# Attention scores in units of two head pairs instead of four heads of one half

## The chip, the cores and the metric

The kernel runs on one core of a Trainium2 chip. The metric is the device time of one execution, in microseconds (us); the median of three runs is given. TensorE is called PE here, VectorE DVE, ScalarE ACT, GpSimd POOL, SyncE SP.

## What is computed

Attention with a band mask and a distance bias, then a feed-forward layer, then an eight-expert layer whose gate is balanced by eight row and column normalisations. The change touches attention alone.

```python
def _attn_ref(q, k, v, n_global, n_local):          # q, k, v: (2, 8, 768, 64) float32
    scores = scale * np.matmul(q, k.transpose(0, 1, 3, 2))
    ...
    keep = is_global | is_local                     # first 8 keys, and the last 96 up to the own one
    bias = -slopes[:, None, None] * dist[None, :, :]
    scores = np.where(keep, scores + bias[None, :, :, :], -1000000000.0)
    a = np.exp(scores - np.max(scores, axis=-1, keepdims=True))
    a = a / (np.sum(a, axis=-1, keepdims=True) + 1e-09)
    return np.matmul(a, v)                          # heads joined: x is (1536, 512)

def _moe_ref(x, w_in, w_out):                       # w_in, w_out: float64
    h = x @ w_in
    return (h * (1.0 / (1.0 + np.exp(-h)))) @ w_out

def _moe2_ref(x, w_gate, w1, w2):
    ...                                             # gate P: exp, then 8 normalisations
    for e in range(E):
        out += P[:, e:e + 1] * (np.maximum(x @ w1[e], 0.0) @ w2[e])
```

## The kernel before, in words

**Attention.** The 1536 tokens are twelve query tiles k of 128. A tile needs 256 keys at most (`W`; 32 places for the global ones and 224 before and up to the query), the first tile of a batch 128. `att_turn` (line 660) transposes a tile's queries and keys on PE, two heads at a time, so that `qT` and `kT` hold the even head of a pair (j = 0) on partitions 0 to 63 and the odd one (j = 1) on partitions 64 to 127. There are four pairs (c). A score product contracts over the 64 rows of one half.

`att_scores(k, j)` (line 708) is a unit: the four heads of half j. For two of them, c and c + 1, it takes one PSUM bank, issues their score products (line 726), and then for each head: DVE adds the table of bias and mask and takes the row's minimum (line 735, tile `s`; the sign of the scores is turned, so that the minimum stands for the maximum), ACT takes the exponential and its sum (line 739); after both heads DVE makes the reciprocals (lines 744 and 745) and POOL scales (line 747). Then it yields. `att_flip` (line 752) transposes a unit's weights on PE, up to four blocks a bank (line 764, tile `a_f`), and copies them to `at`. `att_out` (line 776) multiplies them with the values for a whole tile (line 783, tile `a_o`), and its two copies write x as a rounded part `xh` and a rest `xl`.

Tiles 0 to 7 use fp32 operands (one product for a head, which the trace shows as two matmul records). For tiles 8 to 11 queries and keys are split into a rounded part and a rest, and a head takes three products in fp32r (`qT·kT`, `qT·kTl`, `qTl·kT`), one record each.

**PSUM.** While attention runs there are three banks of tag `a` for all its tiles, taken in turn, one `h` and four `y` (line 846). In the first two tiles the `y` banks serve too.

**Order.** `attention` (line 797) is a generator: each step issues one piece (half a unit's scores, one bank of flips, an `att_out`, a part of a turn). Flips run two units behind the scores (`LAG`). `go` (line 892) runs the first feed-forward layer (`emit_h`, lines 237 to 239 and 256 to 260; `emit_y`, line 276) and lets the generator make a piece each time that its due count reaches one. Each step of that layer is an h (12 matmuls) and a y (12) over 512 tokens; the first token block starts with four steps of half width, twice. The order within an engine is then fixed; the build has moved instructions a little against the order in which the code issues them. Tiles 0 and 1 run ahead of the layer, 2 and 3 in its first steps, 4 to 7 in the rest of token block 0, 8 to 11 in block 1. Block 2 and the second layer (`h_product`, `y_part`) have no attention beside them.

**The weights of block 0.** `w_in` and `w_out` come as float64; `narrow` (line 183) turns a slice of them into fp32 by eight DVE instructions (lines 199 to 205), handed out by `pump` between other work on the same DVE queue. From line 212 on ACT and POOL split them for PE. Blocks 1 and 2 load the fp32 copy.

Of the kernel before, what the change touches and what calls it, by code (L numbers as in the profile page):

```python
# [8 lines left out]
F32 = mybir.dt.float32  # L9
# [5 lines left out]
AF = mybir.ActivationFunctionType  # L15
ALU = mybir.AluOpType
# [4 lines left out]
P = 128  # L21
# [3 lines left out]
W = 2 * P  # L25
BIG = float(2**40)
BIGMIN = 3.0e38
MASKED = 1.0e9
EPS = 1e-9
# [5 lines left out]
LAG = 2  # L35
# [7 lines left out]
def f32(ap):  # L43
    return ap.bitcast(F32)


class Kernel:
# [657 lines left out]
                nc.vector.scalar_tensor_tensor(dst[1], ps, sc, f32(dst[0]), op0=ALU.mult, op1=ALU.subtract)  # L705
            yield

    def att_scores(self, k, j):

        nc, pool = self.nc, self.ap  # L710
        a = self.att[k]
        qT, kT = a["qT"], a["kT"]
        n = W if k % self.QT else P
        jj = slice(j * self.D, (j + 1) * self.D)
        a["s", j] = s = pool.tile([P, 4, W], F32, tag="s", name=f"s_{k}_{j}", bufs=LAG + 1)
        st = pool.tile([P, 3, 4], F32, tag="st", name=f"st_{k}_{j}", bufs=LAG + 2)
        cols = []
        for c in range(self.NPAIR):
            th = self.tab[2 * c + j]
            if c % 2 == 0:  # L720
                bank = self.aps(f"s_{k}_{j}_{c}")
                for x in (c, c + 1):
                    dst = bank[:, x % 2 * W:x % 2 * W + n]
                    ops = ((0, 0), (0, 1), (1, 0))[:3 if len(qT) > 1 else 1]
                    for i, (y, z) in enumerate(ops):
                        nc.tensor.matmul(  # L726
                            dst, qT[y][jj, x * P:(x + 1) * P], kT[z][jj, x, W - n:],
                            start=i == 0, stop=i == len(ops) - 1,
                        )
            ps = bank[:, c % 2 * W:c % 2 * W + n]  # L730
            tt = th[:, :W] if n == W else th[:, W:]
            sx = s[:, c, W - n:]
            cols.append(sx)

            nc.vector.tensor_tensor_reduce(  # L735
                out=sx, in0=ps, in1=tt, scale=1.0, scalar=BIGMIN, op0=ALU.add, op1=ALU.min,
                accum_out=st[:, 0, c:c + 1],
            )
            nc.scalar.activation(
                sx, sx, AF.Exp, bias=st[:, 0, c:c + 1], scale=-1.0, accum_out=st[:, 1, c:c + 1]  # L740
            )
            if c % 2 == 1:
                two = slice(c - 1, c + 1)
                nc.vector.tensor_scalar(st[:, 2, two], st[:, 1, two], EPS, None, op0=ALU.add)  # L744
                nc.vector.reciprocal(st[:, 2, two], st[:, 2, two])
                for y in (c - 1, c):
                    nc.gpsimd.tensor_scalar(
                        cols[y], cols[y], st[:, 2, y:y + 1], 1.0, op0=ALU.mult, op1=ALU.mult
                    )
                yield  # L750

    def att_flip(self, k, j):

        nc, pool = self.nc, self.ap
        a = self.att[k]
        s, blocks = a["s", j], self.blocks(k)
        at = a["at", j] = pool.tile([P, 8 * P], F32, tag="at", name=f"at_{k}_{j}", bufs=2)
        for lo in range(0, len(blocks), 4):
            hi = min(lo + 4, len(blocks))
            ps = self.aps(f"f_{k}_{j}_{lo}")  # L760
            for n in range(lo, hi):
                c, o = blocks[n]
                keys = s[:, c, P:] if o is None else s[:, c, o::2]
                nc.tensor.transpose(ps[:, (n - lo) * P:(n - lo + 1) * P], keys, self.ident)  # L764
            if lo == 0:
                nc.scalar.activation(at[:, :hi * P], ps[:, :hi * P], AF.Copy)
            else:
                self.copy(at[:, lo * P:hi * P], ps[:, :(hi - lo) * P])
            yield

    def blocks(self, k):


        return [(c, o) for c in range(self.NPAIR) for o in ((0, 1) if k % self.QT else (None,))]

    def att_out(self, k):

        nc = self.nc
        a = self.att.pop(k)
        ps = self.aps(f"o_{k}")  # L780
        for n, (c, o) in enumerate(self.blocks(k)):
            for j in range(2):
                nc.tensor.matmul(  # L783
                    ps[j * self.D:(j + 1) * self.D, c * P:(c + 1) * P], a["vw"][:, 2 * c + j, o or 0, :],
                    a["at", j][:, n * P:(n + 1) * P], start=n == 0, stop=o != 0, skip_group_check=True,
                )
        tok = k * P
        xh, xl = (x[:, :, tok % TB:tok % TB + P] for x in self.x1[tok // TB])
        ps = ps.rearrange("p (x c) -> p x c", c=P)
        nc.scalar.activation(xh, ps, AF.Copy)  # L790
        nc.vector.tensor_tensor(xl, ps, f32(xh), op=ALU.subtract)
# [5 lines left out]
    def attention(self, sg):  # L797

        tb = SEGS[sg][0] * P // TB
        if tb not in self.x1:  # L800
            self.x1[tb] = self.new_x(f"x1_{tb}")
        ks = range(*SEGS[sg])
        units = [(k, j) for k in ks for j in range(2)]
        if "qT" not in self.att[ks[0]]:
            yield from self.turn(ks[0])
        none = iter(())
        for u in range(len(units) + LAG + 1):
            v = u - LAG
            if v >= 2 and v % 2 == 0:
                k = units[v - 2][0]  # L810
                self.att_out(k)
                if k + 2 < self.NT // P:
                    self.att_load_v(k + 2)
                yield
            if u % 2 == 0 and u + 2 < len(units):
                yield from self.turn(units[u + 2][0])
            scores = self.att_scores(*units[u]) if u < len(units) else none
            flip = self.att_flip(*units[v]) if 0 <= v < len(units) else none
            n = 1
            while n:  # L820
                n = 0
                for g in (scores, flip):
                    for _ in g:
                        n += 1
                        yield
                        break
# [323 lines left out]
```

## Time and profile before

| | |
|---|---|
| median of 3 runs | 1442.73 us (1442.69 to 1444.27) |
| the profiled execution's own time | 1444.39 us |
| its span, first to last instruction | 1442.6 us |
| mean granted TensorE clock | 0.989 of full |
| PE busy | 1413.3 us, 98% |
| DVE / ACT / POOL busy | 739.9 (51%) / 487.2 (34%) / 553.6 us (38%) |
| score matmuls (line 726) | 224 records, 10.2 to 289.5 us |

The span is read in stretches: 0 to 34 us is tiles 0 and 1 before the layer; to about 158 us the layer's first token block with the narrowing of weights beside it; to about 310 us the rest of attention under the layer; then there is no attention. Matmuls are pipelined, so a matmul's record is longer than its share of the array: the distance between the starts of two matmuls is what the first one costs the stream.

### The profile page before, as it was taken

To read this page: it belongs to the slowest core of one execution; us is meant where nothing else is said; L and a number is where in the kernel's file an instruction comes from. 1 tells how busy PE (TensorE), PEld (TensorE's weight loads), DVE (VectorE), ACT (ScalarE), POOL (GpSimd) and SP (SyncE) were. 2 spreads that over 40 slices of the span, in tenths; PEclk is the share of its full clock that TensorE was granted. 3 is DMA by queue.
4 is the path that set the end of the run, shared out by engine and by line. 5 is a ranking of instruction groups with operands and counts; after the bars stand their busy time and mean duration, and the time that the engine had idled before them with its cause. 6 is when DMAs were issued, how large, how long until landed. Compare 5 with 4: busy or idle time off the path is not lost.

```text
span 1442.6 us, 21250 instructions
## 1 busy us (share of the span) xinstructions
PE 1413.3 (98%) x8552; PEld 1232.1 (85%) x8552; DVE 739.9 (51%) x1298; ACT 487.2 (34%) x949; POOL 553.6 (38%) x489
## 2 busy tenths in 40 slices
PE   8998999999999999999999999999999999999998
PEld 6776687778888989999998999899899899989997
DVE  8899545456353556544354354435444443544443
ACT  6665545555352422222232221223222132322220
POOL 5677755444470423314142331414224141422210
PEclk8899999999999999999999999999999999999999
DMA  9685442222230201011010101102010110201001
GB/s 257 178 245 186 154 121 73 74 74 88 88 103 1 59 1 59 16 44 41 19 50 10 59 16 44 44 16 57 3 59 22 38 45 15 59 0 45 1 28 63
DMA packets 75292, 92.18 MB, mean 64 GB/s; under 512 B 30640, under 2 KB 49072, under 8 KB 75184
## 3 DMA queue, kind: packets, MB, share of 16 engines
q1 hardware_dynamic: 72880, 82.34, 19.2%
q10 hardware_dynamic: 2304, 8.39, 1.5%
q8 instruction: 69, 1.13, 0.3%
q14 instruction: 39, 0.32, 0.1%
HBM read 79.19 MB, written 11.53 MB: 63 GB/s over the span
## 4 chain that ended last, share of the span: by engine, by line
PE 89%; DVE 8%; issue 1%; ACT 1%; POOL 0%; DMA 0%; DVEq 0%; ACTq 0%; SPq 0%; POOLq 0%
PE y L423 37%; PE h L388 32%; PE y L276 7%; PE h L237 3%; PE h L238 3%; PE h L239 3%; PE a_s L726 2%; DVE wf L201 1%; DVE wf L203 1%; DVE wf L199 1%; DVE wf L205 1%; PE a_o L783 1%; PE a_f L764 1%; DVE s L735 1%; DVE st L744 0%
## 5 line engine op out<-in xcount | busy, mean ns | idle before, releaser
L480 DVE TENSOR_TENSOR tabs<-tabs,h 128x512 f32<-128x512 f32 x48 | 33.0, 687 | 333.9 <-PE h L388 333.9
L343 POOL TENSOR_TENSOR wc0l<-wf,wc0h 128x512 fp32r<-128x512 f32 x16 | 21.2, 1323 | 340.3 <-ACT wc0h L342 340.3
L440 DVE SCALAR_TENSOR_TENSOR x<-y,gate,x 128x512 f32<-128x512 f32 x168 | 115.5, 742 | 18.3 <-PE y L423 18.3
L343 POOL TENSOR_TENSOR wx1l<-wf,wx1h 128x512 fp32r<-128x512 f32 x64 | 89.9, 1405 | 79.7 <-ACT wx1h L342 79.5
L402 ACT ACTIVATE room_hh<-tabs 128x512 fp32r<-128x512 f32 x87 | 54.2, 629 | 190.9 <-DVE tabs L410 188.5
L410 DVE TENSOR_TENSOR tabs<-tabs,h 128x512 f32<-128x512 f32 x144 | 98.8, 687 | 19.0 <-PE h L388 16.8
L343 POOL TENSOR_TENSOR wx0l<-wf,wx0h 128x512 fp32r<-128x512 f32 x48 | 62.1, 1293 | 90.3 <-ACT wx0h L342 90.3
L388 PE MATMUL h<-xc,wx1h 128*128 128x256 f32 x512 | 93.4, 280 | 1.7 <-DVE tabs L410 1.7
L388 PE MATMUL h<-xc,wx0h 128*128 128x256 f32 x512 | 93.4, 280 | 0.6 <-DVE tabs L476 0.6
L423 PE MATMUL y<-wx1h,room_hh 128*128 128x512 f32 x232 | 91.2, 393 | 0.0
L423 PE MATMUL y<-wx0h,room_hh 128*128 128x512 f32 x232 | 91.2, 393 | 0.0
L423 PE MATMUL y<-wx0l,room_hh 128*128 128x512 f32 x232 | 90.8, 391 | 0.0
L423 PE MATMUL y<-wx1l,room_hh 128*128 128x512 f32 x232 | 90.8, 391 | 0.0
L423 PE MATMUL y<-wx0h,room_hl 128*128 128x512 f32 x232 | 90.7, 391 | 0.0
L423 PE MATMUL y<-wx1h,room_hl 128*128 128x512 f32 x232 | 90.7, 391 | 0.0
L403 DVE SCALAR_TENSOR_TENSOR room_hl<-tabs,room_hh 128x512 fp32r<-128x512 f32 x87 | 77.6, 898 | 25.5 <-ACT room_hh L402 24.2
L342 ACT ACTIVATE wx1h<-wf 128x512 fp32r<-128x512 f32 x64 | 40.4, 632 | 141.8 <-PE y L423 84.2
L388 PEld LDWEIGHTS h<-xc,wx0h 128*128 128x128 f32 x512 | 82.6, 188 | 5.8 <-DVE tabs L476 0.8
L221 POOL TENSOR_TENSOR w1l<-wf,w1h 128x512 fp32r<-128x512 f32 x48 | 67.0, 1395 | 50.9 <-ACT w1h L220 44.6
L388 PEld LDWEIGHTS h<-xc,wx1h 128*128 128x128 f32 x512 | 80.4, 188 | 4.4 <-DVE tabs L410 1.9
L221 POOL TENSOR_TENSOR w0l<-wf,w0h 128x512 fp32r<-128x512 f32 x48 | 67.0, 1397 | 42.0 <-ACT w0h L220 40.2
L276 PE MATMUL y<-hh,w1h 128*128 128x512 f32 (+1 forms) x208 | 83.0, 399 | 0.0
(270 smaller groups left out, 4143.3 us busy)
## 6 DMA issues: line engine op xcount, KB each, us to landing
wf<-in_moe_w_dram SPq DMA_DIRECT2D x64, 512.0 KB, 3.7
wf<-w SPq DMA_DIRECT2D x32, 512.0 KB, 3.3
ra<-in_moe_w_in_dram SPq DMA_DIRECT2D x16, 512.0 KB, 6.0
rb<-in_moe_w_out_dram SPq DMA_DIRECT2D x16, 512.0 KB, 5.3
w<-wf ACTq DMA_DIRECT2D x16, 512.0 KB, 4.3
vw<-in_v_dram SPq DMA_DIRECT2D x8, 448.0 KB, 4.5
qr<-in_q_dram SPq DMA_DIRECT2D x12, 256.0 KB, 5.8
kr<-in_k_dram SPq DMA_DIRECT2D x12, 256.0 KB, 6.0
```

Of the source, the lines that this page charges most:

```text
L221: nc.gpsimd.tensor_tensor(lo, src, f32(hi), op=ALU.subtract)
L237: nc.tensor.matmul(ps, ah, bh, start=i == 0, stop=False)
L238: nc.tensor.matmul(ps, ah, bl, start=False, stop=False)
L239: nc.tensor.matmul(ps, al, bh, start=False, stop=i == last)
L276: nc.tensor.matmul(self.y[i][:, cols], a, b, start=begin and j == 0, stop=f == self.NF1 - 1 and j == 2, skip_group_check=True,)
L343: self.nc.gpsimd.tensor_tensor(dst[1], src, f32(dst[0]), op=ALU.subtract)
L388: nc.tensor.matmul(ps[:, f * HB:(f + 1) * HB], a[:, k, fs], b[:, k, :], start=first and n == 0, stop=n == 11, skip_group_check=True,)
L402: self.nc.scalar.activation(hi, src, AF.Relu)
L403: self.nc.vector.scalar_tensor_tensor(lo, src, 0.0, f32(hi), op0=ALU.max, op1=ALU.subtract)
L410: self.nc.vector.tensor_tensor(c, a, b, op=op)
L423: nc.tensor.matmul(self.y[i], a, b, start=k == 0 and j == 0, stop=k == 3 and j == 2, skip_group_check=True)
L440: nc.vector.scalar_tensor_tensor(acc, self.y[i], self.gate[:, t, e:e + 1], acc, op0=ALU.mult, op1=ALU.add)
```

## The change

A unit is now two pairs: `att_scores(k, m)` takes the heads of c = 2m and 2m + 1, both halves. It takes two banks at once, one for each half; a bank holds the two heads of its half side by side. All score products of the unit are issued in one piece, and two products of the two halves take turns: for each c and each of its one or three products first j = 0, then j = 1. The reductions then go pair by pair: x = 0 reads both banks, x = 1 again, with a yield after each. The first piece of a unit so holds all its matmuls and two heads' reductions, the second piece the other two heads' reductions and no matmul. `att_flip` and `blocks` count heads of the unit instead of pairs; `att_out` visits the same 16 (or 8) products, ordered by c, key block and j as before, and takes the blocks of c from unit c // 2. The number of instructions of each kind is the same.

```diff
-    def att_scores(self, k, j):
+    def att_scores(self, k, m):
...
-        jj = slice(j * self.D, (j + 1) * self.D)
...
-        for c in range(self.NPAIR):
-            th = self.tab[2 * c + j]
-            if c % 2 == 0:
-                bank = self.aps(f"s_{k}_{j}_{c}")
-                for x in (c, c + 1):
-                    dst = bank[:, x % 2 * W:x % 2 * W + n]
-                    ops = ((0, 0), (0, 1), (1, 0))[:3 if len(qT) > 1 else 1]
-                    for i, (y, z) in enumerate(ops):
-                        nc.tensor.matmul(
-                            dst, qT[y][jj, x * P:(x + 1) * P], kT[z][jj, x, W - n:],
-                            start=i == 0, stop=i == len(ops) - 1,
-                        )
...
+        banks = [self.aps(f"s_{k}_{m}_{j}") for j in range(2)]
+        dst = [bank[:, x * W:x * W + n] for x in range(2) for bank in banks]
+        ops = ((0, 0), (0, 1), (1, 0))[:3 if len(qT) > 1 else 1]
+        for x in range(2):
+            c = 2 * m + x
+            for i, (y, z) in enumerate(ops):
+                for j in range(2):
+                    jj = slice(j * self.D, (j + 1) * self.D)
+                    nc.tensor.matmul(
+                        dst[2 * x + j], qT[y][jj, c * P:(c + 1) * P], kT[z][jj, c, W - n:],
+                        start=i == 0, stop=i == len(ops) - 1,
                     )
-                yield
+        for x in range(2):
+            for h in (2 * x, 2 * x + 1):
+                th = self.tab[4 * m + h]
+                sx = s[:, h, W - n:]
+
+                nc.vector.tensor_tensor_reduce(
+                    out=sx, in0=dst[h], in1=th[:, :W] if n == W else th[:, W:], scale=1.0, scalar=BIGMIN,
+                    op0=ALU.add, op1=ALU.min, accum_out=st[:, 0, h:h + 1],
+                )
...
+            yield
...
     def att_out(self, k):
...
+        for c in range(self.NPAIR):
+            for o in range(keys):
+                for j in range(2):
+                    n = (c % 2 * 2 + j) * keys + o
+                    nc.tensor.matmul(
+                        ps[j * self.D:(j + 1) * self.D, c * P:(c + 1) * P], a["vw"][:, 2 * c + j, o, :],
+                        a["at", c // 2][:, n * P:(n + 1) * P], start=c + o == 0, stop=o == keys - 1,
+                        skip_group_check=True,
+                    )
...
-        units = [(k, j) for k in ks for j in range(2)]
+        units = [(k, m) for k in ks for m in range(2)]
```

**PE, first unit of tile 9 (fp32r, beside y of the layer).** In `a_s_0_0` the first number is the unit; the second is, before, the pair with which the bank begins, and now the half. Before, with the second group of the unit 16 rows further on:

```order
L239 MATMUL h_2415<-x_1xh,w0l_2159 128x512
L726 MATMUL a_s_0_0_2447<-kT_2218,qT_2217 128x256
L726 MATMUL a_s_0_0_2447<-kTl_2220,qT_2217 128x256
L726 MATMUL a_s_0_0_2447<-kT_2218,qTl_2219 128x256
...
L764 MATMUL a_f_0_0_2476<-ident,s_0_2276 128x128 x4
...
L726 MATMUL a_s_0_2_2492<-kT_2218,qT_2217 128x256
L726 MATMUL a_s_0_2_2492<-kTl_2220,qT_2217 128x256
L726 MATMUL a_s_0_2_2492<-kT_2218,qTl_2219 128x256
...
L764 MATMUL a_f_0_4_2523<-ident,s_0_2276 128x128 x4
```

Now:

```order
L239 MATMUL h_2415<-x_1xh,w0l_2159 128x512
L725 MATMUL a_s_0_0_2447<-kT_2218,qT_2217 128x256
L725 MATMUL a_s_0_1_2448<-kT_2218,qT_2217 128x256
L725 MATMUL a_s_0_0_2447<-kTl_2220,qT_2217 128x256
L725 MATMUL a_s_0_1_2448<-kTl_2220,qT_2217 128x256
L725 MATMUL a_s_0_0_2447<-kT_2218,qTl_2219 128x256
L725 MATMUL a_s_0_1_2448<-kT_2218,qTl_2219 128x256
...
L761 MATMUL a_f_0_0_2483<-ident,s_0_2276 128x128 x4
...
L761 MATMUL a_f_0_4_2523<-ident,s_0_2276 128x128 x4
```

Two groups of six in one half have become one group of twelve in which the halves take turns; each head's three products stand twice in a group, for two heads. The program has 45 runs of score products before and 25 now. All eight units of tiles 8 to 11 look like this one.

**PE, tiles 2 and 3 (fp32, beside the first steps of the layer).** The build has put other work between some turns. Before, the score rows alone:

```order
L726 MATMUL a_s_0_0_566<-kT_484,qT_483 128x256 x2
...
L726 MATMUL a_s_0_2_581<-kT_484,qT_483 128x256 x2
L726 MATMUL a_s_1_0_606<-kT_484,qT_483 128x256
...
L726 MATMUL a_s_1_2_625<-kT_484,qT_483 128x256 x2
L726 MATMUL a_s_0_0_646<-kT_512,qT_511 128x256
```

Now, from the second run on:

```order
L725 MATMUL a_s_0_1_567<-kT_484,qT_483 128x256
L725 MATMUL a_s_0_0_566<-kT_484,qT_483 128x256
...
L725 MATMUL a_s_1_0_606<-kT_484,qT_483 128x256
L725 MATMUL a_s_1_1_607<-kT_484,qT_483 128x256
...
L725 MATMUL a_s_0_0_646<-kT_512,qT_511 128x256 x2
...
L725 MATMUL a_s_0_1_647<-kT_512,qT_511 128x256 x2
```

The runs of tiles 2 and 3 hold 2, 3, 4, 1, 2, 1, 1 and 2 heads before and 1, 3, 6, 2 and 4 now; the first unit of tile 3 is torn into its halves, and so is that of tile 4.

**DVE, first unit of tile 2.** Before:

```order
L735 ISA s_0_564,st_0_565<-a_s_0_0_566,tabs 128x256
...
L203 SCALAR_TENSOR_TENSOR wf_554<-ra_330,wf_554 128x512
L257 SCALAR_TENSOR_TENSOR g_523<-g_523,h_474 128x256
L735 ISA s_0_564,st_0_565<-a_s_0_2_581,tabs 128x256
```

Now:

```order
L257 SCALAR_TENSOR_TENSOR g_523<-g_523,h_474 128x256
L734 ISA s_0_564,st_0_565<-a_s_0_0_566,tabs 128x256
...
L734 ISA s_0_564,st_0_565<-a_s_0_1_567,tabs 128x256
...
L203 SCALAR_TENSOR_TENSOR wf_554<-ra_333,wf_554 128x512
```

Two reductions, a narrowing instruction and the layer's g, and two more reductions have become g and four reductions in a row, with the narrowing behind them.

## Rows read from the trace of the kernel before

**Rows 1.** The page, parts 1 and 4: busy time of the engines, and the chain that ended last.

```profile
PE 1413.3 (98%) x8552; PEld 1232.1 (85%) x8552; DVE 739.9 (51%) x1298; ACT 487.2 (34%) x949; POOL 553.6 (38%) x489
...
PE 89%; DVE 8%; issue 1%; ACT 1%; POOL 0%; DMA 0%; DVEq 0%; ACTq 0%; SPq 0%; POOLq 0%
```

**Rows 2.** Table by stretch: length, busy time of each engine, clock, DMA.

```profile
40.00:58.00 18.00, 18.00 (x90) 14.06 (x90) 14.65 (x52) 13.02 (x41) 13.44 (x18) 0.81 0.72 197
58.00:158.00 100.00, 89.86 (x550) 70.71 (x549) 94.08 (x189) 59.62 (x145) 71.25 (x68) 0.97 0.65 198
158.00:200.00 42.00, 40.98 (x224) 32.52 (x223) 11.02 (x30) 22.78 (x47) 27.80 (x29) 1.00 0.41 134
200.00:220.00 20.00, 20.00 (x101) 15.56 (x100) 17.29 (x42) 12.06 (x30) 12.76 (x18) 1.00 0.44 114
220.00:320.00 100.00, 98.93 (x570) 79.03 (x569) 49.73 (x125) 51.84 (x117) 46.83 (x55) 1.00 0.24 75
```

**Rows 3.** Waits of PE from 158 to 420 us: total, times, longest.

```profile
PE h L237 <- DVE g L257: 2.1, 2, 1.1
```

**Rows 4.** Timeline of PE, one fp32r group of tile 11: start, us, what.

```profile
273.37 0.40 PE L276 MATMUL y<-hh,w1l 128*128 128x512 f32 x1
273.69 0.38 PE L726 MATMUL a_s<-kT,qT 64*128 64x256 f32 x1
273.92 0.28 PE L726 MATMUL a_s<-kTl,qT 64*128 64x256 f32 x1
...
274.40 0.28 PE L726 MATMUL a_s<-kT,qTl 64*128 64x256 f32 x1
274.61 0.50 PE L276 MATMUL y<-hh,w1h 128*128 128x512 f32 x1
274.94 0.39 PE L276 MATMUL y<-hl,w1h 128*128 128x512 f32 x1
275.17 0.39 PE L276 MATMUL y<-hh,w1l 128*128 128x512 f32 x1
```

**Rows 5.** Line 726, the product with kTl: shortest/median/longest ns, first and last start.

```profile
L726 PE MATMUL a_s<-kTl,qT x32: 277/277/281, 206.5 to 289.4; 64*128 64x256 f32 x32
```

**Rows 6.** Timeline of PE, one fp32 group of tile 7.

```profile
160.15 0.40 PE L239 MATMUL h<-x_0xh,w0l 128*128 128x512 f32 x1
160.48 1.13 PE L726 MATMUL a_s<-kT,qT 64*128 64x256 f32 x4
...
161.88 0.39 PE L238 MATMUL h<-x_0xl,w0h 128*128 128x512 f32 x1
```

**Rows 7.** Timeline of PE, an fp32 group of four records and one of six.

```profile
57.26 1.13 PE L726 MATMUL a_s<-kT,qT 64*128 64x256 f32 x4
58.31 0.39 PE L237 MATMUL h<-x_0xh,w0h 128*128 128x256 f32 x1
...
78.47 1.13 PE L726 MATMUL a_s<-kT,qT 64*128 64x256 f32 x6
79.53 0.39 PE L237 MATMUL h<-x_0xh,w0h 128*128 128x256 f32 x1
```

**Rows 8.** Waits of DVE for scores, 20 to 60 us, then 158 to 316 us.

```profile
DVE s L735 <- PE a_s L726: 2.4, 4, 1.2
...
DVE s L735 <- PE a_s L726: 18.5, 14, 3.0
```

**Rows 9.** Chain that ended last, first and last of seven score groups, and what follows.

```profile
40.82 2.00 PE a_s L726 x6
...
57.33 1.07 PE a_s L726 x4
...
58.42 0.42 DVE s L735
```

**Rows 10.** Timelines of DVE and PE: a step's g, and the next h.

```profile
188.37 0.69 DVE L257 SCALAR_TENSOR_TENSOR g<-g,h 128x512 f32<-128x512 f32 x1 [4.62 <-ACT g L256]
...
189.96 0.39 PE L237 MATMUL h<-x_0xh,w0h 128*128 128x512 f32 x1
```

More of the change, by code (lines that the diff above doesn't have):

```diff
@@ L713, in att_scores @@
         n = W if k % self.QT else P
-        jj = slice(j * self.D, (j + 1) * self.D)
-        a["s", j] = s = pool.tile([P, 4, W], F32, tag="s", name=f"s_{k}_{j}", bufs=LAG + 1)
-        st = pool.tile([P, 3, 4], F32, tag="st", name=f"st_{k}_{j}", bufs=LAG + 2)
-        cols = []
-        for c in range(self.NPAIR):
-            th = self.tab[2 * c + j]
-            if c % 2 == 0:
-                bank = self.aps(f"s_{k}_{j}_{c}")
-                for x in (c, c + 1):
-                    dst = bank[:, x % 2 * W:x % 2 * W + n]
-                    ops = ((0, 0), (0, 1), (1, 0))[:3 if len(qT) > 1 else 1]
-                    for i, (y, z) in enumerate(ops):
-                        nc.tensor.matmul(
-                            dst, qT[y][jj, x * P:(x + 1) * P], kT[z][jj, x, W - n:],
-                            start=i == 0, stop=i == len(ops) - 1,
-                        )
[L730 to L748, printed above, removed]
-                    )
-                yield
@@ L752, in att_flip @@
-    def att_flip(self, k, j):
+        a["s", m] = s = pool.tile([P, 4, W], F32, tag="s", name=f"s_{k}_{m}", bufs=LAG + 1)
+        st = pool.tile([P, 3, 4], F32, tag="st", name=f"st_{k}_{m}", bufs=LAG + 2)
+        banks = [self.aps(f"s_{k}_{m}_{j}") for j in range(2)]
[9 more added lines that the diff above has]
+                        start=i == 0, stop=i == len(ops) - 1,
+                    )
@@ new lines, in att_scores @@
+        for x in range(2):
[6 more added lines that the diff above has]
+                )
+                nc.scalar.activation(
+                    sx, sx, AF.Exp, bias=st[:, 0, h:h + 1], scale=-1.0, accum_out=st[:, 1, h:h + 1]
+                )
+            two = slice(2 * x, 2 * x + 2)
+            nc.vector.tensor_scalar(st[:, 2, two], st[:, 1, two], EPS, None, op0=ALU.add)
+            nc.vector.reciprocal(st[:, 2, two], st[:, 2, two])
+            for h in (2 * x, 2 * x + 1):
+                sx = s[:, h, W - n:]
+                nc.gpsimd.tensor_scalar(sx, sx, st[:, 2, h:h + 1], 1.0, op0=ALU.mult, op1=ALU.mult)
+            yield
@@ L754, in att_flip @@
+    def att_flip(self, k, m):
         nc, pool = self.nc, self.ap
         a = self.att[k]
-        s, blocks = a["s", j], self.blocks(k)
-        at = a["at", j] = pool.tile([P, 8 * P], F32, tag="at", name=f"at_{k}_{j}", bufs=2)
+        s, blocks = a["s", m], self.blocks(k)
+        at = a["at", m] = pool.tile([P, 8 * P], F32, tag="at", name=f"at_{k}_{m}", bufs=2)
         for lo in range(0, len(blocks), 4):
             hi = min(lo + 4, len(blocks))
-            ps = self.aps(f"f_{k}_{j}_{lo}")
+            ps = self.aps(f"f_{k}_{m}_{lo}")
@@ L761, in att_flip @@
             for n in range(lo, hi):
-                c, o = blocks[n]
-                keys = s[:, c, P:] if o is None else s[:, c, o::2]
+                h, o = blocks[n]
+                keys = s[:, h, P:] if o is None else s[:, h, o::2]
                 nc.tensor.transpose(ps[:, (n - lo) * P:(n - lo + 1) * P], keys, self.ident)
@@ L771, in blocks @@
     def blocks(self, k):
-        return [(c, o) for c in range(self.NPAIR) for o in ((0, 1) if k % self.QT else (None,))]
+        return [(h, o) for h in range(4) for o in ((0, 1) if k % self.QT else (None,))]
     def att_out(self, k):
@@ L780, in att_out @@
         ps = self.aps(f"o_{k}")
[L781 to L786, printed above, removed]
+        blocks = self.blocks(k)
+        keys = len(blocks) // 4
+        for c in range(self.NPAIR):
[6 more added lines that the diff above has]
+                        skip_group_check=True,
+                    )
         tok = k * P
```

## The prediction

> **What bounds the kernel now.** First the page's shares: PE is busy 98% of the span and holds 89% of the chain that ended last [rows 1]. PE's time is the kernel's time wherever nothing else holds it up, so I read next the table by stretch, and of each stretch ask who is full [rows 2]. From 40 to 58 us PE is busy without a gap. From 58 to 158 us DVE has 94.1 of 100 us: it narrows the weights of the first token block, and PE has 10 us idle. From 158 to 320 us PE is full again (159.9 of 162 us) and DVE about half used, except from 200 to 220 us (17.3 of 20). PE's waits confirm it: from 158 to 420 us the list has one entry, 2.1 us in two waits for g [rows 3]. So work taken from PE pays fully after 158 us, partly before 58, and hardly at all between.
>
> **What a score group costs.** The timeline of one fp32r group [rows 4] gives it. Layer matmuls stand 0.23 us apart (274.94 to 275.17). From the last one before the group (273.37) to the second one after (274.94) is 1.57 us; two ordinary distances of 0.23 are 0.46, so the group of six costs 1.11. Inside it the starts are 0.12 apart (273.92 to 274.40 holds four distances), 0.72 for six; the other 0.39 is paid on entering and leaving, when the array changes between all its rows and one half of them. The product with kTl has 32 records [rows 5], two in a group, so there are 16 such groups, all between 206 and 290 us, where PE is full: 17.8 us.
>
> Do two halves run at once? No fp32r row shows it, but fp32 rows do. A group of four records, two heads of one half, takes 1.05 us from its start to the next layer matmul (57.26 to 58.31); a group of six, two heads of one half and then one of the other, takes 1.06 (78.47 to 79.53) [rows 7]. The two records of the other half cost nothing.
>
> **The change part by part.**
>
> *Tiles 8 to 11, fp32r.* Eight groups of twelve take the place of sixteen of six. If each product of j = 1 runs beside that of j = 0, a group has six distances of 0.12 and one entry and exit: 1.11, as before. Eight groups fewer at 1.11: **8.9 us gained**, all on a full PE. If the halves did not overlap, a group would cost 12 x 0.12 + 0.39 = 1.83, and the gain would be 17.8 - 8 x 1.83 = 3.1. I take 8.9, by the rows nearest in kind: the same two halves, the same banks, only another number format.
>
> The Trainium skill would take a little off that: "TensorE: Matmul & The Clock Gate", section "Measured speedup vs the span model", reports 3.07 times, not 4, for four row tiles. If two tiles reached the same three quarters of their ideal, 1.5 times, a group of twelve would be an estimated 1.35 us and the gain 7.0. The six records in the time of four [rows 7] show no such loss, and no run here has four tiles.
>
> *Tile 7, fp32.* Its second unit begins at 160.48. From 160.15 to 161.88 is 1.73 us, less 0.46: a group costs 1.27 [rows 6]. Two become one: **1.25 us gained**.
>
> *Tiles 2 and 3.* From 40.8 to 58.4 us seven of their groups stand in the chain, from 2.00 us at the half clock to 1.07 us [rows 9]; their sum is 8.2. PE is full there and its granted clock 0.81, so part of the stretch ran at the lower of the two levels (1.2 GHz). The build leaves runs of 1, 3, 6, 2 and 4 heads. After the first, two heads of one half cost 1.06 [rows 7], and a run costs its fuller half: 2, 4, 2 and 2 heads, 1.06 + 1.9 + 1.06 + 1.06 = 5.1 at full clock, 7.3 if the first two fall at half (2.0 and some 3.2). That is 0.9 to 3.1 gained on PE. Behind the last group stands a reduction on DVE [rows 9] and then narrowing, so what comes earlier moves DVE earlier. I take **1.5**.
>
> *Tiles 4, 5, 6 and the first unit of 7.* Their groups also shrink, but DVE is 94% busy there [rows 2]. PE idles a little more. I take 0; the ends are the 5.9 us that DVE is idle in that stretch as a gain, and as a loss the same order of time, since DVE's queue is reordered.
>
> *Two banks at once.* The second flip of a unit gets the bank of the first half, which DVE must have read twice by then. In steady tiles PE has 16 matmuls of the layer between the two flips, some 3.7 us at 0.23 [rows 4], and between scores and first flip six more. From 158 to 316 us DVE waited for scores in 14 cases, 18.5 us together [rows 8]: it stands ready when scores come. So 0, except at tile 8, whose two units have no flips between them, in the stretch where DVE is busy 17.3 of 20 us [rows 2]: two groups fewer take 2.2 us from PE there, and DVE has 2.7 left. I take **0.5 lost**, between 0 and 2.2.
>
> *The layer's own wait.* With fewer score matmuls between h and the next h, g may be late. In a step with nothing between, g ends at 189.06 and h starts at 189.96 [rows 10]: 0.9 us to spare even then. Nothing is lost.
>
> *att_out, flips, POOL, ACT, SP:* the same instructions in nearly the same places; `att_out` already let the halves take turns. Nothing.
>
> **The sum.** 8.9 + 1.25 + 1.5 - 0.5 = 11.15 us. The profiled execution took 1444.39 us (span 1442.6), so it would take 1433.2; it lies 1.66 above the median of the runs, 1442.73, from which the same subtraction gives **1431.5 us**.
>
> **The rivals.**
>
> *The halves do not overlap in fp32r.* No row shows that they do; those that do are fp32 [rows 7]. Then tiles 8 to 11 give 3.1 and tile 7 still 1.25, with 0.5 lost and nothing early: 3.85, 1438.9 us. I give it 8%.
>
> *DVE cannot empty two banks in time.* Each unit's second flip, and the next unit's scores, wait for the third and fourth reduction. For it: before, a bank was needed again three pieces after its last reader had been issued, now one. Against it: DVE waits for scores, not PE for DVE [rows 3, 8]. If every one of ten units with flips after 158 us lost 0.5 us, some 5 us would go: 1436.5 us, 8%. A rule of the Trainium skill speaks for this one: "TensorEngine Tiling (Array Packing)", section "PSUM Bottleneck", says that tiling speeds up the matmuls but not the emptying of PSUM, which can become the limit. By that rule the gain would go back to waits; DVE's share of half in the long stretch [rows 2] bears against it.
>
> *DVE's queue is blocked early: slower.* All four reductions of a unit now stand in a row before the narrowing, and they wait for the last score product of the unit. Before, DVE waited for scores 2.4 us in four waits, at most 1.2, between 20 and 60 us [rows 8]. Tiles 2 to 5 have eight units under the narrowing. The loss must exceed the 9.65 us gained after 158 us, so each unit would have to block DVE for over 1.2 us, its longest single wait before, with nothing in between to catch up; at 1.9 us each it is 15 us lost and 1448 us. DVE has enough to do ahead of these reductions to meet the scores, as the first unit's order shows. 4%.
>
> *The change does not do what it says in full.* Tiles 3 and 4 have one unit each torn into its halves by the build, and tile 2 its first turn. This is already in the sum; no group after 158 us is torn.
>
> *The clock.* Before 58 us it was granted 0.81 [rows 2]; an idle moment elsewhere could move the half-clock time by some microseconds either way. This widens the range, and 4% for surprises of that kind that outweigh the rest.
>
> **How the numbers follow.** The forecast has 76%, and within it 1427 to 1436: 1431.5 less the rest of the early gain, or plus an early loss. The range holds 8 in 10 with the second rival's value and most of the first's neighbourhood: 1426.5 to 1438.5. What measurement can tell from no change is 0.2%, 2.9 us, so faster means below 1439.85. The forecast, the bank rival and most of the overlap rival lie there: 0.91. Within 0.2%: the rest of the overlap rival and an early loss that just cancels, 0.05. Slower: the blocked queue, 0.04.
>
> **What would show it.** In the changed profile: score groups of twelve between 200 and 290 us that take 0.9 us from their start to the next layer matmul, with starts of the two halves a few hundredths apart or less; single records still near 277 ns [rows 5]. No wait of PE for a reduction above 1 us after 158 us. The last score group some 10 us earlier, and everything after 320 us merely moved. If groups of twelve take 1.6 us, the overlap fails; if PE's list of waits grows by reductions, the banks; if PE's stretch after 158 us is shorter by 10 us but the total is not, the loss lies before, in DVE's narrowing.

## The result, and the profile after

The changed kernel takes **1432.03 us** (median of 4 runs, 1429.79 to 1432.25) where the kernel before takes 1443.1 in runs beside it (1442.69 to 1444.27): a ratio of 0.9918 over all runs, with an interval of 0.9901 to 0.9936 (the two medians alone give 0.9923). The forecast was 1431.5. The profiled execution took 1432.24 us with a span of 1430.4, 12.15 less than the profiled one of before.

The page, its shares and the chain that ended last, to be read beside [rows 1]:

```profile
PE 1393.2 (97%) x8552; PEld 1218.9 (85%) x8552; DVE 741.2 (52%) x1298; ACT 485.8 (34%) x949; POOL 556.5 (39%) x489
...
PE 87%; DVE 10%; issue 1%; ACT 1%; DMA 0%; POOL 0%; DVEq 0%; SPq 0%; ACTq 0%
```

PE has lost 20.1 us of busy time, DVE has gained two points of the chain. The table by stretch says where, beside [rows 2]:

```profile
40.00:58.00 18.00, 15.48 (x118) 12.74 (x118) 18.00 (x64) 14.52 (x48) 15.26 (x21) 1.00 0.73 201
58.00:158.00 100.00, 84.31 (x527) 67.13 (x523) 94.02 (x190) 60.75 (x147) 75.41 (x71) 0.93 0.65 203
158.00:200.00 42.00, 42.00 (x237) 34.33 (x238) 11.25 (x25) 21.19 (x41) 26.41 (x26) 1.00 0.44 138
200.00:220.00 20.00, 19.94 (x117) 15.47 (x115) 16.43 (x45) 13.09 (x35) 14.04 (x19) 1.00 0.32 83
220.00:320.00 100.00, 98.93 (x591) 80.57 (x590) 50.09 (x122) 53.93 (x120) 49.00 (x56) 1.00 0.28 87
```

After 158 us PE is as full as before, so what was taken from it there came off the time. Before 158 us PE is emptier: from 40 to 58 us DVE is now the full engine (18.00 of 18), and from 58 to 158 us PE has 15.7 us idle instead of 10.1.

To see how much each part gained, follow one instruction that is the same in both: the first h of a layer step (steps are counted from 0). Step 21 opens tile 8's part, step 34 stands behind the last attention. Timeline of PE, kernel before:

```profile
202.18 0.48 PE L237 MATMUL h<-x_1xh,w0h 128*128 128x512 f32 x1
...
310.33 0.40 PE L237 MATMUL h<-x_1xh,w0h 128*128 128x512 f32 x1
```

and the changed kernel:

```profile
198.38 0.48 PE L237 MATMUL h<-x_1xh,w0h 128*128 128x512 f32 x1
...
298.08 0.40 PE L237 MATMUL h<-x_1xh,w0h 128*128 128x512 f32 x1
```

In these two executions 3.80 us are gained up to step 21 (how far that is the change's is asked under e3), and 12.25 up to step 34. Between the two steps lie 108.15 us before and 99.70 now: **8.45 us come from tiles 8 to 11**, where the forecast had 8.9 less 0.5. Behind step 34 nothing changes. One group of tile 11, as in [rows 4]:

```profile
250.83 0.40 PE L239 MATMUL h<-x_1xh,w0l 128*128 128x512 f32 x1
251.16 0.38 PE L725 MATMUL a_s<-kT,qT 64*128 64x256 f32 x2
251.38 0.28 PE L725 MATMUL a_s<-kTl,qT 64*128 64x256 f32 x2
251.50 0.28 PE L725 MATMUL a_s<-kT,qTl 64*128 64x256 f32 x2
251.62 0.28 PE L725 MATMUL a_s<-kT,qT 64*128 64x256 f32 x2
251.73 0.29 PE L725 MATMUL a_s<-kTl,qT 64*128 64x256 f32 x2
251.85 0.29 PE L725 MATMUL a_s<-kT,qTl 64*128 64x256 f32 x2
252.07 0.50 PE L237 MATMUL h<-x_1xh,w0h 128*128 128x512 f32 x1
252.41 0.39 PE L238 MATMUL h<-x_1xl,w0h 128*128 128x512 f32 x1
```

Each row is a pair of products, one of each half, that starts together. From 250.83 to 252.41 are 1.58 us, less 0.46: twelve products cost 1.12 where six cost 1.11.

In the early part a wait has come up that the forecast did not name. PE's waits from 58 to 158 us:

```profile
PE h L237 <- DVE g L257: 11.0, 7, 3.0
PE a_f L761 <- DVE x_1xl L793: 3.9, 1, 3.9
```

The second: of the three banks the first unit of tile 7 takes two at once, one for each half, so the flip that follows, tile 6's first, gets the third, which tile 5's o has held. The last reader of that o is x_1xl, and it stands behind narrowing in DVE's queue. PE stands from 146.8 to 150.7 us. In the kernel before, that bank went to the second group of tile 7's first unit, and its scores waited 1.2 us for the same x_1xl.

### The profile page after: what moved, and what is told of

The parts are those of the page before. It is cut to its first block, busy times and chain, and to the rows that moved or that the text cites. A ratio compares the mean times of both kernels' runs of the same rounds, so it can differ in the third digit from the quotient of the medians.

```text
span 1430.4 us, 21253 instructions
## 1 busy us (share of the span) xinstructions
PE 1393.2 (97%) x8552; PEld 1218.9 (85%) x8552; DVE 741.2 (52%) x1298; ACT 485.8 (34%) x949; POOL 556.5 (39%) x489
## 4 chain that ended last, share of the span: by engine, by line
PE 87%; DVE 10%; issue 1%; ACT 1%; DMA 0%; POOL 0%; DVEq 0%; SPq 0%; ACTq 0%
PE y L423 37%; PE h L388 33%; PE y L276 7%; PE h L237 2%; PE h L238 2%; PE h L239 2%; DVE wf L201 2%; DVE wf L203 1%; DVE wf L199 1%; DVE wf L205 1%; PE a_o L784 1%; DVE s L734 1%; PE a_f L761 1%; DVE st L742 1%; DVE g L257 1%
```

## The experiments

The distance from step 21 to step 34 (read as above) shows the late part without the early one; the median shows both. e1 to e4, e5 to e7 and e8 to e10 each shared a chip and the runs of the kernel before; steps are those of each kernel's profiled execution (e2's took 1436.96 us, 4 under its median). Ratios are over all runs, not of the two medians.

| kernel | median us (lowest to highest, runs) | before beside it | ratio, interval | step 21 at | 21 to 34 |
|---|---|---|---|---|---|
| before | 1443.1 (1442.69 to 1444.27, 4) | | | 202.18 | 108.15 |
| changed | 1432.03 (1429.79 to 1432.25, 4) | 1443.1 | 0.9918, 0.9901 to 0.9936 | 198.38 | 99.70 |
| e1 no turns | 1438.39 (1437.06 to 1439.54, 6) | 1443.62 | 0.9963, 0.9951 to 0.9975 | 200.92 | 101.97 |
| e2 one half | 1440.97 (1436.9 to 1442.19, 12) | 1443.62 | 0.9978, 0.9967 to 0.9988 | 198.02 | 104.89 |
| e3 late only | 1434.32 (1432.54 to 1436.85, 6) | 1443.62 | 0.9939, 0.9926 to 0.9952 | 198.63 | 99.67 |
| e4 early only | 1439.57 (1437.31 to 1439.9, 6) | 1443.62 | 0.9967, 0.9955 to 0.998 | 197.43 | 108.16 |
| e5 o's bank | 1433.13 (1431.99 to 1433.89, 5) | 1444.18 | 0.9921, 0.9907 to 0.9935 | 199.05 | 99.71 |
| e6 thin half | 1431.94 (1431.23 to 1432.72, 5) | 1444.18 | 0.9913, 0.9899 to 0.9926 | 196.75 | 99.28 |
| e7 changed | 1431.01 (1429.01 to 1431.96, 5) | 1444.18 | 0.9908, 0.9894 to 0.9921 | 195.28 | 99.63 |
| e8 rests on DVE | 1416.38 (1416.33 to 1419.17, 5) | 1444.08 | 0.9822, 0.9807 to 0.9837 | 182.44 | 99.85 |
| e9 hl on DVE | 1426.67 (1426.42 to 1426.96, 4) | 1444.08 | 0.9884, 0.9869 to 0.9899 | 192.51 | 99.82 |
| e10 weights' rests on DVE | 1417.15 (1416.82 to 1417.41, 5) | 1444.08 | 0.9817, 0.9804 to 0.9831 | 183.24 | 99.68 |
| e11 before, with e8's edit | 1427.59 (1425.45 to 1428.98, 4) | 1444.12 | 0.9883, 0.9863 to 0.9903 | 185.91 | 108.16 |

### e1: the same units without turns

```diff
-        for x in range(2):
-            c = 2 * m + x
-            for i, (y, z) in enumerate(ops):
-                for j in range(2):
-                    jj = slice(j * self.D, (j + 1) * self.D)
+        for j in range(2):
+            jj = slice(j * self.D, (j + 1) * self.D)
+            for x in range(2):
+                c = 2 * m + x
+                for i, (y, z) in enumerate(ops):
```

> The changed kernel with one edit: a unit still takes two banks and issues all its score products in one piece, but first all products of the lower half (j = 0), then all of the upper (j = 1). Theory A, the array takes up the other half's products as soon as they are queued, whatever their order: groups of twelve still take 0.9 us from their start to the next layer matmul, and the kernel is within 2 us of the changed one (about 11 us faster than before). Theory B, only neighbours in turn overlap: the groups take 1.6 us, 0.72 more in each of eight, 5.8 us, and 0.85 in tile 7; the kernel is only some 4 to 5 us faster than before.

Measured: 1438.39 us, 5.2 under the kernel before and so near theory B's 4 to 5. The groups lie between the two theories: the eight in fp32r take 1.243 to 1.255 us from their start to the layer's next matmul. Timeline of PE, one of them, six products of the lower half issued before six of the upper:

```profile
254.97 0.38 PE L725 MATMUL a_s<-kT,qT 64*128 64x256 f32 x1
255.20 0.28 PE L725 MATMUL a_s<-kTl,qT 64*128 64x256 f32 x1
255.32 0.28 PE L725 MATMUL a_s<-kT,qTl 64*128 64x256 f32 x1
255.32 0.40 PE L725 MATMUL a_s<-kT,qT 64*128 64x256 f32 x2
255.55 0.29 PE L725 MATMUL a_s<-kTl,qT 64*128 64x256 f32 x2
255.66 0.30 PE L725 MATMUL a_s<-kT,qTl 64*128 64x256 f32 x2
255.78 0.28 PE L725 MATMUL a_s<-kT,qT 64*128 64x256 f32 x1
255.90 0.28 PE L725 MATMUL a_s<-kTl,qT 64*128 64x256 f32 x1
256.01 0.28 PE L725 MATMUL a_s<-kT,qTl 64*128 64x256 f32 x1
256.22 0.50 PE L237 MATMUL h<-x_1xh,w0h 128*128 128x512 f32 x1
```

Of the two products in the row at 255.32 that says x2, the first must be the upper half's, since products of one half start 0.12 apart: it was issued seventh and starts with the third. So the halves overlap without turns too, but the upper starts three distances late, 0.35 us, which is 1.25 instead of 0.9. Eight groups make 2.8 us; the distance from step 21 to 34 is 2.3 longer. The rest lies before step 21 (200.92 against 198.38 in the profiles), within the scatter that e3 shows, and was not taken apart. In fp32 the groups of eight records take 1.07 without turns, as with them.

### e2: two groups in one, all of one half

```diff
-            if c % 2 == 0:
-                bank = self.aps(f"s_{k}_{j}_{c}")
-                for x in (c, c + 1):
+            if c == 0:
+                banks = [self.aps(f"s_{k}_{j}_{x}") for x in (0, 2)]
+                for x in range(self.NPAIR):
+                    dst = banks[x // 2][:, x % 2 * W:x % 2 * W + n]
...
```

> The kernel before with one edit: a unit is still four heads of one half, but it takes its two banks at once and issues all its score products in one piece, so there are as few groups as in the changed kernel, and none has products of two halves. Theory of the prediction, the overlap of halves makes most of the gain: a group of twelve takes 12 x 0.12 and stands 1.6 us before the next layer matmul; tiles 8 to 11 gain 3.1 us and tile 7 0.4, so the kernel is 3 to 5 us faster than before. Rival, the gain comes from fewer entries and exits of the half-array mode: groups take 0.9 us and the kernel is some 11 us faster.

Measured: 1440.97 us, with runs from 1436.9 to 1442.2: 2.65 under the kernel before, a little short of the 3 to 5 expected. Groups of twelve in one half take 1.604 to 1.618 us, and the late part is 3.26 us shorter than before. That is the price of eight entries and exits, 0.41 each, where [rows 4] gave 0.39. So of the change's 8.45 us late, 3.3 come from fewer groups and 5.2 from the halves running side by side. Whether the halves could take turns in one bank wasn't tried.

### e3 and e4: one part of the change at a time

```diff
...
-            scores = self.att_scores(*units[u]) if u < len(units) else none
+            k = units[u][0] if u < len(units) else 0
+            score = self.att_scores if k >= 8 else self.att_scores_half
+            scores = score(*units[u]) if u < len(units) else none
```

e3 changes tiles 8 to 11 alone; e4, with the condition turned round, tiles 0 to 7.

> The changed kernel with tiles 0 to 7 (fp32) as before, units of one half, and tiles 8 to 11 (fp32r) as changed. By the two traces, the layer's steps from tile 8 on gained 8.45 us (12.25 at the end of attention less 3.80 at its beginning): 8 to 9 us faster than before, if the two parts add. Rival, the early part alone decides when everything else starts and the late part is given back in waits: under 5 us.

> The changed kernel with tiles 8 to 11 (fp32r) as before and tiles 0 to 7 (fp32) as changed. If the parts add: 2.5 to 4 us faster than before, of which 1.25 is the second unit of tile 7 and the rest what DVE finishes earlier. Rival, the early gain is an accident of one execution: 0 to 2 us.

Measured: 9.3 and 4.05 us under the kernel before. The late parts are exactly the changed kernel's in e3 (99.67) and before's in e4 (108.16). Together 13.35, against 11.07 and 13.17 for the whole change in its two sets of runs: the parts add up within what the runs scatter. e3 has another lesson: its code up to step 21 is that of before, yet its profiled execution reaches step 21 at 198.63, 3.55 us earlier than before's. The granted clock is 0.97 from 40 to 58 us there, and was 0.81 [rows 2]. So the 3.80 us between the first two profiles could be scatter alone. More executions speak for a gain: the changed kernel, e4, e6 and e7 have one and the same code up to step 21 and reach it at 198.38, 197.43, 196.75 and 195.28.

### e5: the wait for o's bank taken away

```diff
-        nc.vector.tensor_tensor(xl, ps, f32(xh), op=ALU.subtract)
+        if self.narrowing:
+            xt = self.ap.tile([P, self.NPAIR, P], F32, tag="xt", name=f"xt_{k}", bufs=1)
+            nc.scalar.activation(xt, ps, AF.Copy)
+            nc.gpsimd.tensor_tensor(xl, xt, f32(xh), op=ALU.subtract)
+        else:
+            nc.vector.tensor_tensor(xl, ps, f32(xh), op=ALU.subtract)
```

> The changed kernel, but while the weights are being narrowed the rest of a piece of o (the subtraction that empties o's bank) is made without VectorE: ScalarE copies o out of its bank into a tile xt, and GpSimd subtracts. Theory: in the changed kernel's trace TensorE stands 3.9 us at 146.8 to 150.7, because tile 7's transposes take the bank of tile 6's o, whose last reader x_1xl stands behind the narrowing in VectorE's queue. Without it that wait is gone, and what it cost on the path comes back: 2.4 to 4 us faster than the changed kernel, 1428 to 1430. Rival: the narrowing itself (VectorE's work up to 151) is the bound there, or GpSimd's narrowing and the subtraction get in each other's way; then the wait turns up in another place and the time stays within 1 us of the changed kernel's, 1431 to 1433.

The tiles named there are one too high: the transposes are tile 6's and the o is tile 5's. Measured: 1433.13 us; e7 beside it takes 1431.01. The gain of the theory is not there, and the rival's mechanism holds; the time lies 2.1 us over e7's, where the rival had 1. The wait for x_1xl is gone, and PE's waits from 140 to 158 us are now this one:

```profile
PE h L237 <- DVE g L257: 5.4, 1, 5.4
```

The next step's g stands behind the same narrowing. In e7, the changed kernel again, PE waited 1.1 us for x_1xl where it waited 3.9 in the first profile; its score group there ran at the lower clock level and took 2.01 instead of 1.06 us, so PE came later to a bank that came free 0.8 us earlier (x_1xl ended at 149.90 us, and at 150.67 in the first profile). In these three executions DVE's queue sets this place, whichever of its instructions PE is waiting for.

### e6: half of the heads with one product instead of three

```diff
-                for j in range(2):
+                for j in range(2 if i == 0 else 1):
...
-                        start=i == 0, stop=i == len(ops) - 1,
+                        start=i == 0, stop=j == 1 or i == len(ops) - 1,
```

Left out, in tiles 8 to 11, are both small-rest products of the upper half's heads.

> The changed kernel, but in tiles 8 to 11 the upper half issues only the first of its three products: the two small-rest products of half the heads are left out there, 8 x 4 = 32 matmuls fewer. If the second half's products run wholly beside the first half's (theory), a group still takes 0.9 us from its first product to the layer's next, and the time is the changed kernel's to within 0.5 us. Rival: the second half's products cost part of their length; then a group gets shorter, by up to 4 x 0.12 = 0.48 us, 3.8 us in all, 1428 to 1429.

Measured: 1431.94 us, and groups of 0.890 to 0.915 us. Timeline of PE:

```profile
249.11 0.38 PE L725 MATMUL a_s<-kT,qT 64*128 64x256 f32 x2
...
250.02 0.50 PE L237 MATMUL h<-x_1xh,w0h 128*128 128x512 f32 x1
```

0.91 us with eight products as with twelve. From step 21 to 34 it is 0.4 us shorter, where the rival had 3.8. The second half's products are free of PE time here. The whole kernel is 0.9 us slower than e7 beside it, where at most 0.5 was expected: from step 34 to its end its profiled execution takes 1133.85 us, the changed kernel's 1132.36; why was not asked.

### e7: the changed kernel again

> The changed kernel itself, on the same chip as the two others: 1430 to 1433, some 11 us under the kernel before. It is there for the two to be compared with.

Measured: 1431.01 us, 13.17 under the kernel before on that chip.

### e8, e9, e10: the subtractions beside the narrowing

e5 left the question why DVE's queue is so slow there. Two timelines of the changed kernel, DVE

```profile
143.06 0.42 DVE L199 TENSOR_SCALAR wf<-ra 128x512 uint32<-128x512 uint32 x1
143.39 1.51 DVE L199 TENSOR_SCALAR wf<-rb 128x512 uint32<-128x512 uint32 x1
144.82 1.77 DVE L201 SCALAR_TENSOR_TENSOR wf<-ra,wf 128x512 uint32<-128x512 uint32 x1
146.51 1.75 DVE L201 SCALAR_TENSOR_TENSOR wf<-rb,wf 128x512 uint32<-128x512 uint32 x1
148.19 0.68 DVE L203 SCALAR_TENSOR_TENSOR wf<-ra,wf 128x512 uint32<-128x512 uint32 x1
```

and POOL

```profile
143.09 1.52 POOL L221 TENSOR_TENSOR w0l<-wf,w0h 128x512 fp32r<-128x512 f32 x1
144.58 1.46 POOL L260 TENSOR_TENSOR hl<-g,hh 128x512 fp32r<-128x512 f32 x1
146.00 1.71 POOL L221 TENSOR_TENSOR w1l<-wf,w1h 128x512 fp32r<-128x512 f32 x1
```

suggest it: while POOL subtracts, each DVE instruction ends a few tenths behind one of POOL's, and takes 1.5 to 1.8 us; without POOL the same kinds take 0.42 and 0.68. e8 moves all these subtractions to DVE, e9 those of h, e10 those of the weights.

```diff
-        nc.gpsimd.tensor_tensor(lo, src, f32(hi), op=ALU.subtract)
+        eng = nc.vector if self.wide and n < self.NF1 else nc.gpsimd
+        eng.tensor_tensor(lo, src, f32(hi), op=ALU.subtract)
...
-        eng = nc.gpsimd if tb == 0 else nc.vector
+        eng = nc.vector
         eng.tensor_tensor(hl, g, f32(hh), op=ALU.subtract)
```

> The changed kernel, but in the first token block the rests of the weights (w0l, w1l) and of the layer's h (hl) are subtracted on VectorE instead of GpSimd. Theory: VectorE's narrowing instructions are stretched (0.68 to 1.5 and 1.8 us) by GpSimd's subtractions beside them. From 58 to 158 us the changed kernel's narrowing has 88 instructions in 76.2 us; at 0.68 (0.415 for line 199) they would take 54.3, so 22 us are lost beside 31 subtractions. Without those on GpSimd the narrowing falls to 54 to 57 us, the 31 subtractions add 31 x 0.68 = 21 on VectorE, and the two cancel: 1429 to 1434. Rival: the stretching comes from elsewhere (transfers, or a weight's arrival). Then narrowing still takes 76 us, the 21 us come on top of a full VectorE, and the time is 1446 to 1452.

> The changed kernel, but in the first token block hl alone is subtracted on VectorE, 12 instructions of 0.68 in the stretch from 58 to 158 us instead of 12 of 1.25 on GpSimd. Theory: each of GpSimd's subtractions costs VectorE 22 / 31 = 0.7 us, so the 8 us added there and the 8.5 saved cancel, and y can begin sooner: 1430 to 1432, at best 1.5 us faster than the changed kernel. Rival: nothing is saved, VectorE has 8 us more: 1436 to 1440.

> The changed kernel, but in the first token block the rests of the weights alone (19 subtractions of 1.58 us on GpSimd between 58 and 158 us) are made on VectorE. Theory: 19 x 0.68 = 13 us added on VectorE, and 19 x 0.7 to 0.9 = 13 to 17 saved: 1428 to 1432. Rival: nothing is saved, 1442 to 1446.

Measured: 1416.38, 1426.67 and 1417.15 us. All three gain more than expected. The stretching does come from POOL's subtractions. Line 201 in e8, shortest, median and longest ns from 58 to 158 us:

```profile
L201 DVE SCALAR_TENSOR_TENSOR wf<-ra,wf x12: 665/683/895, 58.1 to 146.5; 128x512 uint32<-128x512 uint32 x12
```

The longest was 1776 in the changed kernel. Narrowing takes 60.5 us for 95 instructions in that stretch (the groups of DVE's lines added up), where it took 76.2 for 88, and the 37 subtractions add 26.0: DVE's total hardly changes, as expected. What the expectation missed shows in PE's waits: in the changed kernel nearly all of them were for single instructions in DVE's queue, g and x_1xl, and none from 58 to 158 us for one of POOL's subtractions. The stretch and PE's waits in it, e8:

```profile
58.00:158.00 100.00, 97.99 (x625) 77.89 (x625) 98.14 (x250) 73.15 (x174) 34.66 (x42) 1.00 0.72 221
```

```profile
PE a_f L762 <- POOL s L747: 1.1, 1, 1.1
PE h L238 <- DVE g L258: 0.8, 2, 0.5
```

PE is idle 2.0 us instead of 15.7 and has the full clock, which was 0.93. How much each of these makes of the gain was not separated, nor was the build's order, which changes on all engines with this edit; nor do the parts add: e9 and e10 take 5.4 and 14.9 us off the changed kernel's first median, e8 15.7. e8 is the fastest kernel of the study: 15.7 us under the changed kernel's first median, 27.7 under the kernel before on its chip.

### e11: the kernel before with the edit of e8

> The kernel before with the edit of the run e8 alone: in the first token block the rests of weights and h are subtracted on VectorE, units of four heads of one half as before. Theory: the stretching of the narrowing by GpSimd's subtractions has nothing to do with the change, so it goes here too, and the two edits add up: the e8 kernel's 1416.4 plus at least the 8.4 us of tiles 8 to 11, whose groups are sixteen of six again: 1424.8. With TensorE full (98 of 100 us) from 58 to 158 us in that kernel, earlier groups that are single again cost their part too, up to 5 us more: 1425 to 1430. Rival: the two are the same gain taken twice, the narrowing's end being set by TensorE's speed: then this kernel is within 3 us of e8, 1416 to 1419, or it gains nothing over before, 1441 to 1445.

Measured: 1427.59 us. The theory holds: 16.5 us under the kernel before beside it, and 11.2 over e8. Of these, 8.31 are the distance from step 21 to 34 (108.16 against 99.85). PE is idle 0.4 us from 58 to 158 us in e11, so earlier groups count there as well; but in e8 the build leaves many early units torn into groups of four, and up to step 21 the two are 3.47 us apart, no more than the scatter of that part in e3. So the change is worth about the same with and without DVE's stretching: 11.2 us here, 11.1 and 13.2 there.

## Why the prediction was right

*The sum.* 11.15 us were forecast; the medians differ by 11.07, the profiled executions by 12.15, and e7 by 13.17. Taken off the median of before, 1442.73, each gives a time inside the range (the forecast's own subtraction gives 1431.58, not 1431.5). That it came within 1 us is luck in part: the early terms are smaller than the 3.55 us by which two executions of the same code differ up to step 21.

*Tiles 8 to 11: 8.9, the step that carried the sum.* A group cost 1.12 where 1.11 was forecast, and e2 and e6 show both halves of its reasoning: eight entries and exits are worth 3.3 us, and the second half's products cost nothing. The row that it was taken from, six fp32 records in the time of four [rows 7], was a good guide to another number format.

The Trainium skill's figure for four row tiles ("TensorE: Matmul & The Clock Gate", section "Measured speedup vs the span model") had given an estimated 1.35 us for a group. The trace has 0.9 us to the next matmul and a cost of 1.12, so for two halves that loss does not appear.

*Tile 7: 1.25.* From step 15 to step 16 are 9.70 us before (159.59 to 169.29) and 8.37 now (157.12 to 165.49): 1.33.

*Tiles 2 and 3: 1.5.* This can't be read off one pair of profiles. Step 4 begins at 70.71 us in before, at 66.82 and 66.08 in the two profiles of the changed kernel; but at 67.18 in e3, whose code is before's up to there. Most of the 3.9 us in the first pair so came with the execution, not with the groups: before ran at a granted clock of 0.50 from 40 to 46 us, e3 at 0.91, and PE had waited 2.3 us for x_0xl in before and 0.7 in e3. By medians, each against the kernel before beside it, the early part with tile 7 is worth 1.8 to 3.9 us (the whole change less e3) and 4.05 (e4), where 2.75 was forecast. The term is of the right size, and no finer statement is shown.

*Tiles 4 to 6: nothing.* Held in the sum, for a reason that was only half told. DVE's queue does set that stretch. What came earlier on PE turned into waits: from 36 to 166 us PE waits 12.0 us for g in the changed kernel and 9.2 in before, and 3.9 for x_1xl where before had 1.2. Step 14 begins 5.29 us earlier than before and step 15 only 2.47. That the two score banks shift which bank a flip gets, and so tie it to an x_1xl behind narrowing, was missed. So was POOL's part in the length of the narrowing, which e8 shows.

*Two banks at tile 8: 0.5 lost.* Eight groups at 1.11 are 8.88, and 8.45 were gained: 0.43, so the size is right. The place is right in part: step 22, beside tile 8's second unit, gains 0.90 where the other steps with a group fewer gain 1.07 to 1.14. The reason given is not shown. PE's waits from 158 us to 420 have one entry for g, 1.1 us, against 2.1 in [rows 3], and none is for a reduction. What stands at the end of step 22 is g, DVE and then PE:

```profile
212.16 0.67 DVE L257 SCALAR_TENSOR_TENSOR g<-g,h 128x512 f32<-128x512 f32 x1
...
212.43 0.40 PE L276 MATMUL y<-hh,w1l 128*128 128x512 f32 x1
212.89 0.50 PE L237 MATMUL h<-x_1xh,w0h 128*128 128x512 f32 x1
```

The h starts 0.46 us behind the last y instead of 0.23, right after g has ended. So 0.23 us were lost in the layer's own wait, of which the forecast said that it loses nothing.

*The rivals.* No overlap would have made groups of 1.6 us; only e2, which forbids overlap, has them. Emptying two banks cost PE nothing after 158 us, so the page "TensorEngine Tiling (Array Packing)" of the Trainium skill, section "PSUM Bottleneck", warns of a limit that this kernel doesn't reach there. The queue blocked early did not come about as told: DVE's waits from 20 to 60 us and from 58 to 158 us have no entry for scores any more (e7's have one, 1.5 us), where before had 2.4 and 0.8 us. What was lost early, the 2.8 us between steps 14 and 15, PE lost by waiting for DVE's queue.

## What to carry to other kernels

Where a product uses half of the array's rows, issue the products of the two halves in turn and into two banks: in this kernel the second half was free, and every entry into and exit from half the rows that was saved was worth some 0.4 us besides. Where PE waits on a queue, look at the length of the instructions ahead of the one it waits for, and at what another engine does while they are long: the wait in e5 only moved to its neighbour, and taking POOL's subtractions away gave more than the whole change. A gain in a stretch whose clock varies can't be read from one pair of profiles; measure it between two fixed instructions where the clock is full.

## What the runs showed of the hardware that was not expected

**Products of the other half overtake.** In e1 the upper half's first product, issued seventh, starts at 255.32 with the lower half's third, and ahead of three that were issued before it. In fp32 the fifth of eight starts with the first. In both it starts beside one issued four places ahead, so without turns a short group overlaps wholly and a long one in part.

The Trainium skill says under "TensorE: Matmul & The Clock Gate", section "The mechanism", that matmuls start and end strictly in the order of issue; the rows of e1 show another order of starts.

**DVE is stretched by POOL.** Narrowing instructions take 1.5 to 1.8 us beside POOL's subtractions and 0.42 or 0.68 without; POOL's own take 1.46 to 1.71. Moving those subtractions onto the fuller engine made the kernel 15.7 us faster.

The Trainium skill's page "SBUF — State Buffer", section "Who interferes with whom", says that a VectorE instruction with two inputs from SBUF contends with a GpSimd instruction that reads SBUF, and that the later one waits for the whole of the other. The trace agrees for line 201, whose 1.77 us end 0.55 us behind POOL's hl. Line 199, a tensor_scalar, has a single input and is stretched as well, from 0.42 to 1.51; the section says that this operation, too, can contend, in a mode that takes both pairs of ports, and no run shows whether line 199 ran in it.

**The early part scatters, and the lower clock level falls in different places.** The same code up to step 21 took 202.18 us in one profiled execution (before) and 198.63 in another (e3), with a granted clock of 0.81 and 0.97 from 40 to 58 us. The clock is one difference between the two; that it makes the whole of the 3.55 us is not shown. What decides which stretch is granted the lower level was not tried.
